# The due time of four early loads of w2 in a planned schedule: 240 becomes 300

## The chip, the core and the metric

One core of a Trainium2 chip runs the whole kernel; the metric is the device time of one execution in microseconds (us), lower is better. The time before is the median of 3 executions, 1378.37 us (1377.45 to 1378.69).

## What is computed

`x` is 2048 x 1024 in float32. Two sublayers follow each other, each behind an adaptive layer norm:

```python
h = _layernorm(x) * (1 + ca) + sa
x = x + ga * Real(DFT_seq(DFT_hidden(h)))          # first half
h = _layernorm(x) * (1 + cb) + sb
y = _layernorm(h)
x = x + gb * (gelu(y @ w1 + b1) @ w2 + b2)         # second half; w1: 1024 x 3584, w2: 3584 x 1024
```

The six rows sa ... gb are `silu(c) @ w_mod`.

## The kernel before

**The work.** The function `fast` does the first half with folded Fourier matrices and the second half as a Strassen-like scheme: w1 and w2 are cut into 14 pairs of columns or rows, and each product of a 2 x 2 block of such operands is made of 7 products, numbered m = 0 to 6 and taken in the order 0, 1, 2, 4, 3, 6, 5. Every operand is split into a high and a low float16 part, and one product is 12 matmuls of 128 x 512 (three passes by four). "gemm3 g" is the product with pair g of w1 (line 3628, 7 products, then a gelu), "gemm4 v" the one with pair v of w2 (line 3742, two blocks of 7 products, added up in SBUF). After the first gemm3 products the program is: gemm3 0, 1, 2, gemm4 0, gemm3 3, 4, gemm4 1 and so on up to gemm4 13.

**Preparing w1 and w2.** Before pair g of w1 or v of w2 can be used, its raw rows are loaded, four squares with a sum on ScalarE (line 3311), an all-reduce on GpSimd (L3323) and small VectorE instructions (L3319 to 3341) find its scale, and then 14 or so instructions split it: the high part on ScalarE (L2379), the low part (L2391) and combinations (L2405) on VectorE. The same lines split the gelu's output ("hid g"). Their third operand tells them apart: `s1c` is w1, `s2c` is w2, `shc` is hid. Operands for the first three pairs of w1 are made early, stored in HBM (`fw`), and loaded back ("reloads": L3480 for pairs 0 and 1, L3487 for pair 2) when their places come free. For pair 0 of w2 the rows are loaded twice: by `early2` (L3494, four loads of 512 KB) into a place that is free early, and only the squares read them; and by `raw2(0, q)` (L3497, four loads of 512 KB) into the place from which they are split. The raw rows of pairs 3 and 4 of w1 come by L3491 (four loads of 256 KB).

**What else runs there.** The end of the first half and the second half's layer norms overlap with this. A tile i of 128 rows is made by PE (L3046, L3058), assembled by VectorE (L3068, L3073), gets its residual (L3138 and L3139 for the last four tiles, whose x came by L3101), is stored to the output by SP (L3148, "x1 i"), goes through squares on ScalarE (L3120), small root steps (L2620, L2621, L2626 to 2629), two VectorE scalings (L3158, L3162) and a ScalarE scaling (L3171), is transposed on PE (L3181, "turn i"), copied (L3185) and split (L3211 high, L3220 low, L3233 combinations); GpSimd stores the splits of the second half of the tiles ("z", L3226, `fzc`). The pieces of the last eighth ("z7") pass through the place into which `raw2(1, q)` (L3296, rows of pair 1 of w2) is loaded next. L2894 and L2926 load w_mod's columns and b2 for the row gb, and L2900 multiplies it.

**How the order is set.** Nothing is ordered by hand: tasks with an engine, an assumed cost, dependences and a due time stand in streams, and a planner emits each engine's program in its own idea of time. Each engine then runs its program strictly in order, SP too, which issues all its loads and stores in the emitted order and waits at each for what it needs. Among a queue's tasks that are ready at once the planner takes the one with the earlier due time (`pick_first`). So a due time moves not only its own task, but all that is planned behind it, on all engines.

```python
for g, n in ((3, 2), (3, 3), (4, 0), (4, 1)):
    load(("raw1", g, n), f, [("P", 15), ("Q", 15)], 0.75, "rw2", 250.0)      # L3491
for q in range(4):
    load(("early2", q), f, [("P", 15), ("Q", 15)], 1.5, "rw3", 240.0)        # L3494
for q in range(4):
    load(("raw2", 0, q), f, [("turn", 13)], 1.5, "rw2", 240.0)               # L3497
```

P 15 and Q 15 are the products of the last tile of the first half.

Of the kernel before, what the change touches and what calls it, by code (L numbers as in the profile page):

```python
# [17 lines left out]
P = 128  # L18
# [1973 lines left out]
def fast(ctx, tc, x, cre, cim, dre, dim, w1, b1, w2, b2, c, wm, out):  # L1992
# [29 lines left out]
    def FA(off, *dims, p0=0, pn=P):  # L2022
        return view(arena32, off, dims, p0, pn)
# [104 lines left out]
    def raw1(g, n):  # L2128
        return at(raw1_at(g, n), 512)

    def raw2(v, q):
        return at(O_K + 4 * q, 1024).rearrange("p (s x) -> p s x", s=2)
# [314 lines left out]
    def add(stream, eng, cost, fn, deps=(), key=None, due=0.0, tag=None):  # L2447
        t = Task(eng, cost, fn, deps, key)
        push(stream, tag or stream, [t], due)
        return t.key  # L2450
# [38 lines left out]
    def load(name, f, deps=(), cost=1.4, stream="ld", due=0.0):  # L2489
        return add(stream, "dma", cost, f, deps, name, due)  # L2490
# [362 lines left out]
    for cls in range(2):  # L2853
        f = lambda cls=cls: gp.memset(FA(SPB[cls], (1, 1026), pn=64), 0.0)
# [228 lines left out]
    for n in range(2):  # L3083
        f = lambda n=n: gp.memset(FA(QS[n] + 256, (1, 1)), 0.0)
# [288 lines left out]
    def early2(q):  # L3373

        return at(144 + 4 * q, 1024).rearrange("p (s x) -> p s x", s=2)
# [114 lines left out]
    for g, n in ((3, 2), (3, 3), (4, 0), (4, 1)):  # L3490
        f = lambda g=g, n=n: sp.dma_start(raw1(g, n), w1[g, :, PLACE.index(n), :])  # L3491
        load(("raw1", g, n), f, [("P", 15), ("Q", 15)], 0.75, "rw2", 250.0)
    for q in range(4):
        f = lambda q=q: sp.dma_start(early2(q), w2[0:2, :, q, :].rearrange("j p x -> p j x"))  # L3494
        load(("early2", q), f, [("P", 15), ("Q", 15)], 1.5, "rw3", 240.0)
    for q in range(4):
        f = lambda q=q: sp.dma_start(raw2(0, q), w2[0:2, :, q, :].rearrange("j p x -> p j x"))  # L3497
        load(("raw2", 0, q), f, [("turn", 13)], 1.5, "rw2", 240.0)
# [523 lines left out]
def kernel(tc, *args):  # L4022
    odd = fast(tc, *args)
    with tc.If(odd > 0):
        general(tc, *args)
# [46 lines left out]
```

## Time and profile before

| what | value |
|---|---|
| median of 3 executions | 1378.37 us |
| profiled execution | 1377.23 us |
| its span, first to last instruction | 1375.4 us |
| TensorE matmul (PE) busy | 1291.3 us, 94% |
| VectorE (DVE) busy | 1088.4 us, 79% |
| ScalarE (ACT) busy | 746.6 us, 54% |
| moved to and from HBM | 306.22 MB, mean 223 GB/s |
| mean granted TensorE clock | 0.972 |

All times of the profile count from the first instruction. The execution lies 1.8 us outside the span (1377.23 - 1375.4). A row of a timeline gives start, length, engine, line, operation, and in brackets the idle time of the engine just before it and what ended that. PE is the matmul engine, SP's queue (SPq) issues loads and stores; a row of SPq is the issue, not the transfer. "x12" counts instructions merged in a row.

### The profile page before, as it was taken

The numbers are of one execution on the slowest core, as the hardware profiler recorded it, in microseconds if no ns is written. First come the engines' busy times: TensorE is split into PE (matmuls) and PEld (weight loads), VectorE is DVE, ScalarE is ACT, GpSimd is POOL, SyncE is SP. The second block draws the span as 40 slices with busy tenths as digits, with TensorE's granted clock in tenths as the row PEclk, the third lists the DMA queues.
The fourth block names the chain that finished last, engine by engine and source line by source line (L and its number), as shares of the span: only waits on it lengthen the run. The fifth ranks groups of instructions, "written<-read, shape, count | busy, mean of one in ns | idle before, by whom it ended". The sixth has DMA issues, their size and how long they took to land.

```text
span 1375.4 us, 17329 instructions
## 1 busy us (share of the span) xinstructions
PE 1291.3 (94%) x6081; PEld 622.9 (45%) x6081; DVE 1088.4 (79%) x1623; ACT 746.6 (54%) x1188; POOL 265.1 (19%) x426
## 2 busy tenths in 40 slices
PE   5888899777989999999999999999999999999997
PEld 1445466543434444444444444444444444444443
DVE  5888789998588999898989996566685858687695
ACT  4476557877667747474746433256545353636330
POOL 2000010102102000000000000254553433553201
PEclk9888899998999999999999999999999999999999
DMA  9777046569536957575453555999797878786524
GB/s 368 307 250 231 1 169 169 133 194 381 218 145 200 320 146 226 171 204 187 153 184 130 200 205 223 262 349 338 252 318 240 296 264 294 268 306 235 176 81 111
DMA packets 109754, 306.22 MB, mean 223 GB/s; under 512 B 14076, under 2 KB 14076, under 8 KB 107736
## 3 DMA queue, kind: packets, MB, share of 16 engines
q1 hardware_dynamic: 76776, 197.73, 40.5%
q0 software_dynamic: 32880, 107.29, 25.9%
q8 instruction: 49, 0.80, 0.2%
q14 instruction: 49, 0.40, 0.1%
HBM read 220.03 MB, written 84.93 MB: 222 GB/s over the span
## 4 chain that ended last, share of the span: by engine, by line
PE 67%; DVE 9%; ACT 4%; issue 2%; DMA 2%; SPq 0%; POOL 0%; DVEq 0%; ACTq 0%; POOLq 0%
PE ps L3742 34%; PE ps L3628 32%; ACT arena L2379 1%; DVE arena L2391 1%; DVE arena L3220 1%; DVE arena L2405 1%; DVE arena L3162 1%; PE ps L3046 1%; DVE arena L3233 1%; DMA arena<-fw 1%; DMA fzc<-arena 1%; ACT arena L3211 1%; DVE arena L3792 0%; DMA arena<-in_w_dram 0%; PE ps L3058 0%
## 5 line engine op out<-in xcount | busy, mean ns | idle before, releaser
L3628 PE MATMUL ps<-arena 128*128 128x512 f16 x2352 | 515.5, 381 | 9.4 <-DMA arena<-fw 4.8
L3742 PE MATMUL ps<-arena 128*128 128x512 f16 x2352 | 513.2, 380 | 8.0 <-ACT arena L3782 6.2
L3628 PEld LDWEIGHTS <-arena 128*128 128x128 f16 x2352 | 230.8, 98 | 289.9 <-issue 10.8
L3742 PEld LDWEIGHTS <-arena 128*128 128x128 f16 x2352 | 230.7, 98 | 288.3 <-issue 12.0
L3792 DVE SCALAR_TENSOR_TENSOR arena<-ps,i4c,arena 128x1024 f32<-128x1024 f32 x179 | 229.5, 1282 | 104.9 <-PE ps L3742 100.4
L2379 ACT ACTIVATE arena<-arena,shc 128x512 f16<-128x512 f32 (+1 forms) x115 | 115.8, 1017 | 137.2 <-DVE arena L2405 80.3
L2391 DVE SCALAR_TENSOR_TENSOR arena<-arena,shc 128x512 f16<-128x512 f32 (+1 forms) x115 | 129.0, 1121 | 29.6 <-ACT arena L2379 29.2
L2405 DVE TENSOR_TENSOR arena<-arena 128x512 f32<-128x512 f32 (+1 forms) x196 | 148.5, 764 | 3.7
L3533 ACT ACTIVATE arena<-arena 128x512 f32<-128x512 f32 (+5 forms) x148 | 91.2, 617 | 108.8 <-DVE arena L3542 84.8
L3647 ACT ACTIVATE arena<-arena,b1s,i1c 128x512 f32<-128x512 f32 x78 | 63.4, 813 | 90.0 <-DVE arena L3654 88.1
L2379 ACT ACTIVATE arena<-arena,s1c 128x512 f16<-128x512 f32 (+1 forms) x70 | 60.9, 886 | 66.5 <-DVE arena L2405 42.2
L3654 DVE TENSOR_TENSOR arena<-arena,ps 128x512 f32<-128x512 f32 x78 | 53.4, 685 | 52.4 <-PE ps L3628 51.7
L3542 DVE TENSOR_TENSOR arena<-arena 128x256 f32<-128x256 f32 x240 | 87.9, 421 | 1.7 <-DMA arena<-in_cre_dram 1.7
L3323 POOL PARTITION_ALL_REDUCE sums<-sums x21 | 10.4, 501 | 405.0 <-DVE sums L3319 405.0
L3559 POOL DMA_DIRECT2D arena<-in_cim_dram x99 | 54.5, 551 | 92.3 <-ACT arena L3533 86.1
L2391 DVE SCALAR_TENSOR_TENSOR arena<-arena,s1c 128x512 f16<-128x512 f32 (+1 forms) x70 | 65.8, 958 | 5.0 <-ACT arena L2379 4.9
L3559 POOL DMA_DIRECT2D arena<-in_cre_dram x99 | 54.6, 552 | 68.3 <-ACT arena L3533 50.9
L3650 ACT ACTIVATE arena<-ps 128x512 f32<-128x512 f32 x78 | 45.8, 588 | 35.8 <-PE ps L3628 35.6
L2391 DVE SCALAR_TENSOR_TENSOR arena<-arena,s2c 128x1024 f16<-128x1024 f32 x49 | 62.0, 1279 | 0.9 <-ACT arena L2379 0.9
L3046 PE MATMUL ps<-arena 128*128 128x256 f16 (+3 forms) x400 | 51.7, 290 | 10.1 <-DVE arena L3073 10.1
L2900 PE MATMUL ps<-arena,scol 128*128 128x512 f32 x128 | 58.3, 602 | 0.3 <-ACT arena L2915 0.3
L2379 ACT ACTIVATE arena<-arena,s2c 128x1024 f16<-128x1024 f32 x49 | 55.0, 1137 | 5.8 <-DVE arena L2405 5.8
(204 smaller groups left out, 1230.7 us busy)
## 6 DMA issues: line engine op xcount, KB each, us to landing
fw<-arena SPq DMA_DIRECT2D x71, 512.0 KB, 5.0
arena<-fw SPq DMA_DIRECT2D x119, 256.0 KB, 4.9
arena<-fw SPq DMA_DIRECT2D x49, 512.0 KB, 7.0
arena<-in_cre_dram POOLq DMA_DIRECT2D x96, 256.0 KB
arena<-in_cim_dram POOLq DMA_DIRECT2D x96, 256.0 KB
arena<-in_wm_dram SPq DMA_DIRECT2D x32, 512.0 KB, 7.5
arena<-in_w_dram SPq DMA_DIRECT2D x32, 512.0 KB, 6.4
arena<-in_w_dram SPq DMA_DIRECT2D x56, 256.0 KB, 4.5
```

The lines of the kernel that those rows point to most:

```text
L2379: act.activation(o[m][0], q(j), AF.Copy, **sc)
L2391: dve.scalar_tensor_tensor(o[m][1], q(j), scale, o[m][0], op0=ALU.mult, op1=ALU.subtract)
L2405: dve.tensor_tensor(q(d), q(a), q(b), op=op)
L2900: pe.matmul(bank((6 if n < 3 else 4) + h), scol[:, k : k + 1].to_broadcast([P, P]), FA(o + 512 * h, (1, 512)), start=k == 0, stop=k == 7,)
L3046: pe.matmul(PA(pb + o, (1, w)), l, r, start=n == 0, stop=n == len(mm_) - 1)
L3533: f = lambda: act.activation(sq(a), sq(a), AF.Square, accum_out=csum[0:pn, n : n + 1])
L3542: dve.tensor_tensor(a[:, o::2], a[:, o::2], b[:, o::2], op=op)
L3559: return lambda t: gp.dma_start(t[0:pn], v)
L3628: pe.matmul(ps.rearrange("p (k t) -> p k t", k=4), w1c[:, m, s, a, d * P : (d + 1) * P], zc(m)[:, b, :, d, :], start=(start and d == 0 and ...
L3647: act.activation(dst, src, AF.Gelu_apprx_tanh, scale=inv, bias=b1s[:, 2 * p + j : 2 * p + j + 1])
L3742: pe.matmul(t[:, j], hidc[:, c_, m, a, k * P : (k + 1) * P], w2c[:, m, c_, w], start=(start and c_ == 0 and n == 0), stop=(c_ == 1 and n = ...
L3792: lambda: dve.scalar_tensor_tensor(dst, ps[b], inv, dst, op0=ALU.mult, op1=ALU.add), kp[b],
```

## The change

One number: the due time of the four early loads of w2's rows goes from 240 to 300, behind that of the raw rows of w1 (250) and of all other loads that are planned there.

```diff
     for q in range(4):
         f = lambda q=q: sp.dma_start(early2(q), w2[0:2, :, q, :].rearrange("j p x -> p j x"))
-        load(("early2", q), f, [("P", 15), ("Q", 15)], 1.5, "rw3", 240.0)
+        load(("early2", q), f, [("P", 15), ("Q", 15)], 1.5, "rw3", 300.0)
```

No instruction is added to or taken from PE; the planner's orders change on all engines from P 15 on. Three places matter.

**SP's queue around the reloads.** These are SP's rows from the load of the last x tiles (L3101) on: first before, then of the change. L3491 are w1's raw rows, L3494 the early rows of w2, L3148 the stores of x1 13 and then x1 14 and 15, L3487 and L3480 the reloads, L2894 and L2926 the loads for gb.

```order
L3494 DMA arena_65<-in_w_dram 128x2x512
L3101 DMA arena_65<-in_x_dram 128x2x1024
L3494 DMA arena_65<-in_w_dram 128x2x512 x3
L3491 DMA arena_65<-in_w_dram 128x512 x2
L3148 DMA out_dram<-arena_65 128x1024
L3491 DMA arena_65<-in_w_dram 128x512 x2
L3487 DMA arena_65<-fw_2_78 128x1024
L3480 DMA arena_65<-fw_0_76 128x1024
L2894 DMA arena_65<-in_wm_dram 128x1024 x5
L3480 DMA arena_65<-fw_1_77 128x1024
L3148 DMA out_dram<-arena_65 128x1024
L2926 DMA arena_65<-in_b_dram 128x1024
```

```order
L3491 DMA arena_65<-in_w_dram 128x512 x2
L3494 DMA arena_65<-in_w_dram 128x2x512 x3
L3148 DMA out_dram<-arena_65 128x1024
L3494 DMA arena_65<-in_w_dram 128x2x512
L3487 DMA arena_65<-fw_2_78 128x1024
L3148 DMA out_dram<-arena_65 128x1024
L3480 DMA arena_65<-fw_0_76 128x1024
L2894 DMA arena_65<-in_wm_dram 128x1024 x5
L3480 DMA arena_65<-fw_1_77 128x1024
L3480 DMA arena_65<-fw_0_76 128x1024
L3480 DMA arena_65<-fw_1_77 128x1024
L2926 DMA arena_65<-in_b_dram 128x1024
```

The second piece begins one load after the first: ahead of it stand two L3491 and the same L3101. The early rows of w2 now follow w1's raw rows, and, which the due time does not say, the store of x1 14 has moved ahead of the reload for product 2 of gemm3 0 (the first L3480 here), and two more reloads (product 3) ahead of b2. Behind these rows the store of x1 15 stands ahead of the next reloads, L3487 x2 and L3480 x6, where before it stood behind the first four L3480 of them.

**ScalarE around the four squares of w2 pair 0.** These are ACT's rows from L3171 of tiles 10 and 11 on, before and then of the change. L3311 are the squares, L3928 the copies of gemm3 0's products, L3120 the squares of tiles 12 and 13.

```order
L3311 ACTIVATE arena_65,sums_2197<-arena_65 128x1024
L3211 ACTIVATE arena_65<-arena_65 128x2x512
L3211 ACTIVATE arena_65<-arena_65 128x512
L3120 ACTIVATE arena_65,lns_21_141<-arena_65,lns_21_141 128x1024 x2
L3185 ACTIVATE arena_65<-ps 128x1024
L3928 ACTIVATE arena_65<-ps 128x512
L3211 ACTIVATE arena_65<-arena_65 128x2x512
L3185 ACTIVATE arena_65<-ps 128x1024
L2620 ACTIVATE lns_21_141<-lns_21_141,eps_13_114 128x2
L2621 ACTIVATE lns_21_141<-lns_21_141,eps_13_114 128x2
L3311 ACTIVATE arena_65,sums_2197<-arena_65 128x1024 x3
L3120 ACTIVATE arena_65,lns_21_141<-arena_65,lns_21_141 128x1024 x2
```

```order
L3120 ACTIVATE arena_65,lns_21_141<-arena_65,lns_21_141 128x1024
L3185 ACTIVATE arena_65<-ps 128x1024
L3928 ACTIVATE arena_65<-ps 128x512
L2620 ACTIVATE lns_21_141<-lns_21_141,eps_13_114 128x2
L2621 ACTIVATE lns_21_141<-lns_21_141,eps_13_114 128x2
L3211 ACTIVATE arena_65<-arena_65 128x2x512
L3311 ACTIVATE arena_65,sums_2282<-arena_65 128x1024
L3928 ACTIVATE arena_65<-ps 128x512
L3120 ACTIVATE arena_65,lns_21_141<-arena_65,lns_21_141 128x1024 x2
L2620 ACTIVATE lns_21_141<-lns_21_141,epsz_115 128x2
L2621 ACTIVATE lns_21_141<-lns_21_141,epsz_115 128x2
L3311 ACTIVATE arena_65,sums_2282<-arena_65 128x1024
```

One square and not four stands ahead of the second L3120 x2, and the copy of product 2 (the second L3928), which waits for PE, has moved ahead of them; before it stood behind them.

**VectorE ahead of gemm4 0.** These are the DVE rows that end with the first L3792, which adds up gemm4 0's second product, before and then of the change.

```order
L2391 SCALAR_TENSOR_TENSOR arena_65<-arena_65,s1c_147 128x512
L3654 TENSOR_TENSOR arena_65<-arena_65,ps 128x512
L2391 SCALAR_TENSOR_TENSOR arena_65<-arena_65,shc_149 128x2x512
L2391 SCALAR_TENSOR_TENSOR arena_65<-arena_65,s1c_147 128x512
L2405 TENSOR_TENSOR arena_65<-arena_65 128x1024
L2405 TENSOR_TENSOR arena_65<-arena_65 128x512
L2391 SCALAR_TENSOR_TENSOR arena_65<-arena_65,s2c_151 128x2x512 x2
L2405 TENSOR_TENSOR arena_65<-arena_65 128x1024 x2
L2391 SCALAR_TENSOR_TENSOR arena_65<-arena_65,s2c_151 128x2x512 x3
L3792 SCALAR_TENSOR_TENSOR arena_65<-ps,i4c_152,arena_65 128x2x512
```

```order
L2391 SCALAR_TENSOR_TENSOR arena_65<-arena_65,s2c_151 128x2x512
L3654 TENSOR_TENSOR arena_65<-arena_65,ps 128x512
L2405 TENSOR_TENSOR arena_65<-arena_65 128x1024 x2
L3319 TENSOR_REDUCE sums_2710<-sums_2710 128x1
L3327 TENSOR_SCALAR sums_2710<-sums_2710 128x1
L3349 COPY f2c_146<-sums_2710 128x1
...
L2391 SCALAR_TENSOR_TENSOR arena_65<-arena_65,s2c_151 128x2x512 x3
L3792 SCALAR_TENSOR_TENSOR arena_65<-ps,i4c_152,arena_65 128x2x512
L2391 SCALAR_TENSOR_TENSOR arena_65<-arena_65,s1c_147 128x512 x2
L2405 TENSOR_TENSOR arena_65<-arena_65 128x512
```

Three instructions for pair 3 of w1 (two `s1c` and the last L2405 of 512) no longer stand between or ahead of the last parts of w2 pair 0; they come behind L3792. On ACT the two `s1c` go behind the first L3782 (which takes gemm4 0's first product out of PSUM) in the same way, and only three instead of five `s2c` stand together right ahead of L3782. On PE, product 4 of gemm3 0 goes ahead of turn 13, products 0 and 1 of gemm3 1 go behind turn 14, and product 3 of gemm3 1 goes behind turn 15.

## Prediction

> **What bounds the kernel now.** I began with the busy shares by stretch (start:end, length, then PE, PEld, DVE, ACT and POOL busy with instruction counts, granted clock, DMA share, GB/s).
>
> ```profile
> span 1375.4 us, 17329 instructions
> ...
> 300.00:320.00 20.00, 15.56 (x59) 7.94 (x58) 16.84 (x25) 15.62 (x24) 4.84 (x7) 0.82 1.00 349
> 320.00:340.00 20.00, 14.51 (x53) 6.74 (x51) 19.35 (x39) 16.78 (x26) 5.92 (x9) 0.95 1.02 365
> 340.00:360.00 20.00, 18.25 (x82) 8.53 (x83) 8.69 (x19) 8.53 (x16) 2.61 (x4) 0.88 0.89 348
> 400.00:500.00 100.00, 94.18 (x423) 41.93 (x423) 85.62 (x133) 67.02 (x88) 14.28 (x20) 0.97 0.78 239
> 500.00:700.00 200.00, 200.00 (x928) 90.68 (x927) 180.64 (x245) 117.38 (x154) 9.84 (x15) 1.00 0.60 187
> ```
>
> From 500 us on PE has no idle time, so what the change saves or loses before that passes to the end one to one. From 300 to 340 the DMA engines are full (1.00, 1.02) while PE is not. Then I read PE's timeline and its waits.
>
> ```profile
> 312.04 5.28 PE L3628 MATMUL ps<-arena 128*128 128x512 f16 x12 [3.29 <-DVE arena L3073]
> ...
> 322.07 2.76 PE L3628 MATMUL ps<-arena 128*128 128x512 f16 x12 [1.09 <-DMA arena<-fw]
> 324.67 3.60 PE L2900 MATMUL ps<-arena,scol 128*128 128x512 f32 x8
> ...
> 329.58 5.32 PE L2900 MATMUL ps<-arena,scol 128*128 128x512 f32 x12
> 336.93 1.09 PE L3181 MATMUL ps<-ident,arena 128*128 128x128 f32 x8 [2.03 <-ACT arena L3185]
> 341.75 17.25 PE L3628 MATMUL ps<-arena 128*128 128x512 f16 x72 [3.73 <-DMA arena<-fw]
> ...
> 404.50 20.87 PE L3742 MATMUL ps<-arena 128*128 128x512 f16 x84 [6.21 <-ACT arena L3782]
> ```
> ```profile
> 444.19 26.22 PE L3628 MATMUL ps<-arena 128*128 128x512 f16 x120 [0.70 <-ACT arena L3650]
> 471.04 5.34 PE L3628 MATMUL ps<-arena 128*128 128x512 f16 x24 [0.62 <-ACT arena L3650]
> 476.21 24.12 PE L3742 MATMUL ps<-arena 128*128 128x512 f16 x111
> ```
>
> The last big stop is 6.21 us ahead of 404.50 (product 2 of gemm4 0); the one ahead of 341.75 is the wait for the reload of product 4 of gemm3 0. A full-speed matmul is 24.12/111 = 0.217 us, a product 2.61. The 72 at 341.75 should take 15.6 and take 17.25 (1.6 lost), the 84 at 404.50 18.25 and take 20.87 (2.6 lost), and the 12 at 312.04 take twice their time: a stop of 3.3 us or more costs 1.6 to 2.6 on top.
>
> Why the 6.21? The queue that PE waited for:
>
> ```profile
> 398.97 2.48 DVE L2405 TENSOR_TENSOR arena<-arena 128x1024 f32<-128x1024 f32 x2
> 401.41 3.68 DVE L2391 SCALAR_TENSOR_TENSOR arena<-arena,s2c 128x1024 f16<-128x1024 f32 x3
> ```
> ```profile
> 400.23 3.23 ACT L2379 ACTIVATE arena<-arena,s2c 128x1024 f16<-128x1024 f32 x3 [3.10 <-DVE arena L2405]
> 403.36 1.09 ACT L3782 ACTIVATE arena<-ps,i4c 128x1024 f32<-128x1024 f32 x1
> ```
>
> L3782 frees gemm4 0's first bank. It stands on ACT behind the last splits of w2 pair 0, these wait for combinations on DVE, and DVE is late because it prepared hid 0, hid 1, w2 pair 0 and part of pair 3 of w1 in one run.
>
> **Term A: PE's entry into gemm4 0.** No PE instruction is added, so I count PE's work from T, the start of product 4 of gemm3 0 (341.75 before). In the changed order 11 products (28.7), three transpositions of 8 (turn 13 now lies behind T; 1.0 each by the row at 336.93, 3.0) and the slow start (1.6), then 7 products of gemm3 2 (18.3) and 2 of gemm4 0 (5.2) follow: product 2 of gemm4 0 at T + 56.8. This holds if DVE and ACT keep up, which I take them to do: L3782 has three splits, not five, right ahead, and three pair-3 instructions on DVE go behind, two narrow L2391 and one narrow L2405 (next starts follow some 0.1 us inside the lengths of these rows, so 0.66 + 0.66 + 0.6, about 1.9 us):
>
> ```profile
> 391.17 0.75 DVE L2391 SCALAR_TENSOR_TENSOR arena<-arena,s1c 128x512 f16<-128x512 f32 x1
> ...
> 437.29 0.68 DVE L2405 TENSOR_TENSOR arena<-arena 128x512 f32<-128x512 f32 x1
> ```
>
> Before, the same place was reached at 404.50 + 2.6 = 407.1 in full-speed terms. With T unchanged A is 407.1 - 398.55 = 8.5.
>
> **T itself.** These rows of SP's queue, with the landing that the chain of waits gives, and one of ACT and DVE:
>
> ```profile
> 317.78 0.38 SPq L3480 DMA_DIRECT2D arena<-fw  x1
> ...
> 328.49 0.34 SPq L3148 DMA_DIRECT2D out_dram<-arena  x1
> ...
> 332.44 4.29 SPq L3480 DMA_DIRECT2D arena<-fw  x4
> 337.59 0.34 SPq L3148 DMA_DIRECT2D out_dram<-arena  x1
> ```
> ```profile
> 332.44 9.26 DMA arena<-fw
> ```
> ```profile
> 317.36 0.60 ACT L3928 ACTIVATE arena<-ps 128x512 f32<-128x512 f32 x1 [2.52 <-PE ps L3628]
> ...
> 323.48 1.13 ACT L3120 ACTIVATE arena<-arena,lns 128x1024 f32<-128x1024 f32 x1
> ...
> 325.87 0.29 ACT L2620 ACTIVATE lns<-lns,epsz 128x2 f32<-128x2 f32 x1
> ```
> ```profile
> 326.30 0.16 DVE L2626 RECIPROCAL lns<-lns 128x2 f32<-128x2 f32 x1
> ...
> 328.98 0.68 DVE L3073 TENSOR_TENSOR arena<-ps,arena 128x512 f32<-128x512 f32 x1
> ...
> 331.50 1.22 DVE L3138 TENSOR_TENSOR arena<-arena 128x1024 f32<-128x1024 f32 x1
> ...
> 335.74 1.22 DVE L3139 SCALAR_TENSOR_TENSOR arena<-arena 128x1024 f32<-128x1024 f32 x1
> ```
>
> The four early loads and the four L3491 change places, which by bytes is nothing (both sets still stand ahead of all reloads). But the store of x1 14 (issued 328.49) now precedes the reload of product 2 (317.78), and the store of x1 15 (337.59) that of product 4 (332.44). A store is 512 KB, 1.5 us at the 349 GB/s of its stretch. So product 2, which waits for its reload alone, comes about 1.8 us later (one issue, one store): 323.9 to 326.5. Its copy now stands ahead of the squares L3120 that began at 323.48, so tiles 12 to 15 shift by about 3 us: copy 0.5, two squares 2.3, roots 0.4, the small DVE steps 1.0, L3073 0.6, L3138 1.1, L3139 1.2 end the tile 15 that x1 15 waits for, 7.1 us behind product 2, and with the issues ahead the reload of product 4 goes out 8.4 behind it: 334.9 instead of 332.44. It needs no more waiting than before, and two reloads (product 3) have left its front. Lower bound for T: turn 12 waits for the same chain (5.5 us behind product 2), then 1.1 and the 5.32 of L2900: 326.5 + 11.9 = 338.4. Upper bound: product 2 starts after a stop of 2.9 us; if that costs what the 3.29 at 312.04 did, it ends at 329.2, the reload goes out at 337.6 and with the 9.26 lands at 346.9. Since the DMA engines are full either way I take the old T plus one store, T = 343.25, and keep 338.4 and 346.9. **A is 407.1 - 400.05 = 7.0.**
>
> The page "TensorE: Matmul & The Clock Gate" of the Trainium skill (Part 1) says that the clock falls to half after an idle window of about 3.4 us; by that the 2.9 us cost nothing more and the upper end of T is 344.3. The trace has halving at 3.29 and none at 2.03 (336.93), so no row here decides it.
>
> **Term B: DVE up to gemm4 1.** Rows of the next piece, and SP's wait:
>
> ```profile
> 422.32 1.83 DVE L3220 TENSOR_TENSOR arena<-arena 128x1024 f16<-128x1024 f32 x2
> ...
> 441.04 0.16 DVE L3319 TENSOR_REDUCE sums<-sums 128x1 f32<-128x4 f32 x1 [3.08 <-ACT ps L3311]
> ...
> 474.62 1.28 DVE L2391 SCALAR_TENSOR_TENSOR arena<-arena,s2c 128x1024 f16<-128x1024 f32 x1
> ...
> 479.00 1.28 DVE L3792 SCALAR_TENSOR_TENSOR arena<-ps,i4c,arena 128x1024 f32<-128x1024 f32 x1 [1.11 <-PE ps L3742]
> ```
> ```profile
> 439.86 1.03 ACT L3311 ACTIVATE ps<-arena 128x1024 f32<-128x1024 f32 x1 [1.05 <-DMA arena<-in_w_dram]
> ```
> ```profile
> SPq L3296 <- DMA fzc<-arena: 8.3, 2, 7.8
> ```
>
> The rows of w2 pair 1 can be loaded only when z7's stores have left the same place; z7 ends on DVE at 424.1, the last square waits for its load until 439.86, and DVE stops until 441.04. From there to the end of w2 pair 1's last part (475.82) DVE works almost without a gap, 34.8 us. z7's last pieces stand behind the fourth L3782 in both orders, so they move with PE, by A: DVE resumes at 441.04 - 7.0 = 434.0. But in the changed order more stands between: counted in the two orders, one wide and one narrow L2391, two narrow L2405 and one norm's five small steps of some 0.15 (1.2 + 0.66 + 1.2 + 0.75 = 3.8). So the last part ends at 434.0 + 34.8 + 3.8 = 472.6, and the first evacuation of gemm4 1, which stands behind it on DVE (L3792, 1.2), at 473.8. PE wants that bank for product 2 of gemm4 1 at 400.05 + 26 products (67.8) + 5.2 = 473.05. It waits 0.75, and a stop so short shows no slow clock. Before, there were 0.70 and 0.62 of such stops in this piece; I leave them in. B is -0.5 to -0.75; bounds: 0, and -7.7, if z7's stores land no earlier than before (441.04 + 38.6 + 1.2 = 480.8 against 473.05). I take -0.5, nearer the first, as the chain to z7 goes through PE.
>
> **Sum:** 7.0 - 0.5 = 6.5 us. The profiled execution of 1377.23 (span 1375.4 + 1.8) would become 1370.7; it lies 1.1 below the median, so the median of 1378.37 becomes 1371.9.
>
> **Rivals.** *The gain is given back at gemm4 1.* DVE, 86% busy from 400 to 500, prepares w2 pair 1 later than before, and w1 pair 4 and hid 2 ahead of it. For it: the waits through z7's stores have 7.8 us in one piece. Against it: DVE still idles 3.08 there. With B at 5 to 7.7 the time is 1376.5 to 1379, no change.
> *Slower: the reload of product 2.* Each us that it lands late is passed on, through the copy, the squares, tile 15, x1 15 and SP, to the reload of product 4. It landed 4.3 us after its issue (317.78 to 322.07). If it takes the 9.26 that the other took, product 2 starts at 327.4, ends slow at 332.7, the next reload goes out at 341.1 and lands at 350.4; with the last x tiles' load another 1 to 2 us late, T is 352 and A is -1.7. From T = 352.5 on (6.5 + 2.75 later than my T) it is a loss that counts: 1381 to 1382. For it: DMA share 1.00. Against it: only 512 KB more stand ahead.
> The page "DMA: Bandwidth & Descriptors" (Queues, rings and completion order) of the Trainium skill says that each engine consumes a queue's descriptors in ring order and takes turns between queues; it speaks for this rival. By it the store ahead costs at least its bytes; the 9.26 at 332.44 agrees with a queue, 4.3 at 317.78 with a short one.
> *The loads go earlier than T needs.* If two reloads fewer in front and the idle SP let product 4's land at once, T is 338.4 and A 11.9; B stays, since z7 and DVE move with PE: 1367.
>
> **How the numbers follow.** Forecast and its surroundings (T 340 to 346) 0.60, early T 0.10, gain given back 0.16, slower 0.14. A measurement tells about 0.2% (2.75 us) from no change. Faster 0.70, the same 0.16, slower 0.14. The range takes T from 338.4 to 346.9 with B from 0 to -5: 1366.5 to 1379.5.
>
> **What would show it.** Right: no stop of 6 us ahead of product 2 of gemm4 0, PE there at about 400; the wait for the reload of product 4 ends at 340 to 346; product 2 of gemm3 0 starts 1 to 3 us later; the last square of w2 pair 1 starts about 433; PE stops under 1.5 us at product 2 of gemm4 1. Wrong: a PE stop over 3 us between 405 and 480, or after 500; T beyond 350; a stop at gemm4 0 as before, which would mean that DVE's work and not its order made it.

## The result, and the profile after

The change makes the kernel faster: a median of 1369.96 us (1367.97 to 1370.92, 4 executions) against 1377.91 of the kernel before (1377.30 to 1378.69, 4 executions), ratio 0.9949 with a 95% interval of 0.9931 to 0.9967. The forecast was 1371.9. The profiled execution took 1370.08 us. On a second chip, with more executions, the kernel before spread from 1370.1 to 1379.2 (31, median 1375.0), the change from 1368.5 to 1373.0 (10, median 1370.4): ratio 0.9957, 0.9941 to 0.9973. The gain is real, and it is nearer to 5 us than to the 8 of the first medians.

The profile of the change, busy shares by stretch (columns as in the prediction):

```profile
span 1368.1 us, 17330 instructions
...
300.00:320.00 20.00, 12.11 (x47) 5.87 (x45) 19.41 (x33) 13.89 (x21) 4.84 (x7) 0.81 1.03 375
320.00:340.00 20.00, 16.66 (x40) 6.96 (x40) 11.98 (x20) 13.66 (x23) 2.76 (x4) 0.76 0.84 295
340.00:360.00 20.00, 17.68 (x88) 8.77 (x89) 13.54 (x29) 15.83 (x22) 6.21 (x10) 1.00 1.02 371
400.00:500.00 100.00, 97.24 (x452) 43.86 (x451) 86.97 (x134) 63.91 (x84) 15.09 (x21) 1.00 0.79 229
500.00:700.00 200.00, 200.00 (x928) 90.62 (x927) 182.65 (x249) 122.65 (x161) 9.34 (x15) 1.00 0.62 195
```

From 400 to 500 PE is busy 97.24 instead of 94.18 and the clock is whole. PE's timeline at the places of the prediction (the first row is the last product of tile 15):

```profile
292.59 4.13 PE L3046 MATMUL ps<-arena 128*128 128x257 f16 x24 [3.15 <-DVE arena L3073]
...
320.93 5.29 PE L3628 MATMUL ps<-arena 128*128 128x512 f16 x12 [3.87 <-DMA arena<-fw]
...
341.29 2.76 PE L3628 MATMUL ps<-arena 128*128 128x512 f16 x12 [1.50 <-DMA arena<-fw]
...
361.04 5.34 PE L3628 MATMUL ps<-arena 128*128 128x512 f16 x24 [1.84 <-ACT arena L3928]
...
398.62 31.24 PE L3742 MATMUL ps<-arena 128*128 128x512 f16 x144 [0.29 <-ACT arena L3782]
429.70 36.42 PE L3628 MATMUL ps<-arena 128*128 128x512 f16 x168
...
474.06 6.22 PE L3742 MATMUL ps<-arena 128*128 128x512 f16 x28 [2.76 <-DVE arena L3792]
```

The 6.21 ahead of product 2 of gemm4 0 is 0.29, and the 144 matmuls behind it run at full speed. The two small stops of the kernel before (0.70 in gemm3 3, 0.62 in gemm3 4) are gone too. Two new stops stand at 361.04 and at 474.06 (product 2 of gemm4 1).

**A trap in this comparison.** Up to the products of tile 15 both programs are the same, yet this profile is 2.45 us early there. Here is the same row of the kernel before, and then of a repetition of the change (the second view ended at 300 and holds 21 of the 24 matmuls):

```profile
295.04 5.30 PE L3046 MATMUL ps<-arena 128*128 128x257 f16 x24 [3.15 <-DVE arena L3073]
```
```profile
295.64 4.66 PE L3046 MATMUL ps<-arena 128*128 128x257 f16 x21 [3.15 <-DVE arena L3073]
```

Over the 14 profiles of this study that row starts anywhere from 290.17 to 295.64, whichever kernel runs. So I count each profile from there: "the stretch" is the span less the start of that row, and a place "at +46.7" lies 46.7 us behind it. Before, the stretch is 1375.4 - 295.04 = 1080.36 (repeated: 1080.31); of the change 1368.1 - 292.59 = 1075.51 (repeated: 1371.1 - 295.64 = 1075.46). **By these profiles, two of each kernel, the change is worth 4.85 us**; the other 2.45 of the 7.3 between the two spans belong to the execution. One thing stays open: the fastest execution of the kernel before on the second chip has a span of 1368.3, and with a stretch of 1080.3 the shared row would lie at 288.0 there, earlier than in any profile. So some executions of the kernel before probably have a shorter stretch than its two profiles.

### The profile page after: what moved, and what is told of

Its sections match the earlier page's. It is cut to its first block, busy times and chain, and to the rows that moved or that the text cites. A ratio compares the mean times of both kernels' runs of the same rounds, so it can differ in the third digit from the quotient of the medians.

```text
span 1368.1 us, 17330 instructions
## 1 busy us (share of the span) xinstructions
PE 1285.2 (94%) x6081; PEld 620.1 (45%) x6081; DVE 1089.1 (80%) x1623; ACT 748.2 (55%) x1188; POOL 263.8 (19%) x426
## 4 chain that ended last, share of the span: by engine, by line
PE 67%; DVE 10%; DMA 3%; ACT 2%; issue 2%; SPq 1%; POOL 0%; DVEq 0%; POOLq 0%; ACTq 0%
PE ps L3742 34%; PE ps L3628 31%; DVE arena L2391 2%; DVE arena L3220 1%; DVE arena L3162 1%; DVE arena L2405 1%; ACT arena L2379 1%; DMA arena<-in_w_dram 1%; PE ps L3046 1%; DVE arena L3233 1%; DMA arena<-in_wm_dram 1%; PE ps L3058 1%; DMA frow_gbb<-arena 0%; DVE arena L3654 0%; PE ps L3181 0%
## 5 line engine op out<-in xcount | busy, mean ns | idle before, releaser
L3792 DVE SCALAR_TENSOR_TENSOR arena<-ps,i4c,arena 128x1024 f32<-128x1024 f32 x179 | 229.4, 1282 | 103.0 <-PE ps L3742 101.0
L2405 DVE TENSOR_TENSOR arena<-arena 128x512 f32<-128x512 f32 (+1 forms) x196 | 148.9, 764 | 3.7
L3654 DVE TENSOR_TENSOR arena<-arena,ps 128x512 f32<-128x512 f32 x78 | 53.4, 685 | 51.6 <-PE ps L3628 50.9
L2900 PE MATMUL ps<-arena,scol 128*128 128x512 f32 x128 | 61.5, 630 | 2.7 <-DMA arena<-in_wm_dram 2.4
L3311 ACT ACTIVATE ps<-arena 128x1024 f32<-128x1024 f32 x46 | 46.7, 1016 | 19.0 <-DMA arena<-in_w_dram 9.6
```

Of the source, the lines that this page charges most:

```text
L2405: dve.tensor_tensor(q(d), q(a), q(b), op=op)
L2900: pe.matmul(bank((6 if n < 3 else 4) + h), scol[:, k : k + 1].to_broadcast([P, P]), FA(o + 512 * h, (1, 512)), start=k == 0, stop=k == 7,)
L3792: lambda: dve.scalar_tensor_tensor(dst, ps[b], inv, dst, op0=ALU.mult, op1=ALU.add), kp[b],
```

## The experiments

My theory after the result: DVE's order ahead of the first evacuation of gemm4 0 made the stop of 6.21, the pieces of pair 3 above all, and part of the gain is given back at gemm4 1, where DVE has too much to do. The rivals: the loads alone make the gain through T; or the difference is in the execution.

In the table, T is the start of product 4 of gemm3 0; "entry" is the start of product 2 of gemm4 0; the stops are those at product 2 of gemm4 0 and of gemm4 1, with a star where PE ran at half clock for some us behind it. Ratios are to the kernel before on the same chip, whose medians beside e1 to e4, e5 to e8 and e9 to e12 were 1375.0, 1374.7 and 1375.1. Where no entry is given, no stop marks the place in PE's merged rows.

| run | median us (executions) | ratio, 95% | T | entry | stops | stretch |
|---|---|---|---|---|---|---|
| before | 1377.91 (4) | | +46.71 | +109.46 | 6.21*, none | 1080.36 |
| change | 1369.96 (4) | 0.9949, 0.9931 to 0.9967 | +48.70 | +106.03 | 0.29, 2.76 | 1075.51 |
| e1 | 1370.41 (10) | 0.9957, 0.9941 to 0.9973 | +47.80 | +105.98 | 0.28, 2.75 | 1075.46 |
| e2 | 1373.46 (10) | 0.9989, 0.9969 to 1.001 | +45.75 | +105.46 | 3.87*, 2.75* | 1078.26 |
| e3 | 1376.46 (10) | 1.001, 0.9992 to 1.0029 | +48.43 | +110.80 | 5.18*, none | 1080.17 |
| e4 | 1372.29 (10) | 0.9974, 0.9956 to 0.9992 | +47.50 | | none, 3.23* | 1075.50 |
| e5 | 1365.89 (4) | 0.9929, 0.9909 to 0.995 | +46.51 | +104.23 | 0.29, none | 1071.03 |
| e6 | 1366.89 (4) | 0.9929, 0.9904 to 0.9954 | +48.96 | | none, none | 1073.57 |
| e7 | 1377.30 (1) | | +47.06 | +109.65 | 6.21*, none | 1080.31 |
| e8 | 1370.64 (9) | 0.9964, 0.9948 to 0.9981 | +47.55 | +104.85 | 0.28, 2.75* | 1075.90 |
| e9 | 1372.39 (10) | 0.9967, 0.9951 to 0.9984 | +47.10 | +105.31 | 0.29, 2.75* | 1076.33 |
| e10 | 1368.81 (5) | 0.9947, 0.9924 to 0.997 | +48.72 | +106.28 | 0.29, none | 1073.19 |
| e11 | 1366.43 (5) | 0.9942, 0.9919 to 0.9965 | +45.71 | | none, none | 1071.80 |
| e12 | 1366.90 (6) | 0.9947, 0.9928 to 0.9965 | +45.17 | | none, none | 1070.56 |

**e1, the change again** (no edit).

> The changed kernel once more, to see how much of its 7.3 us between the two profiles is the change. Up to the products of tile 15 both programs are the same, yet the profile of the change stood 2.45 us earlier there (SP's load at the same place of the queue 297.06 against 299.51, PE L3046 292.59 against 295.04). Theory: that part is a difference of one execution and not of the change, so the same place comes between 292.5 and 295.1 in this profile, and behind it the rows are the same to 0.5 us: the stop ahead of product 2 of gemm4 0 under 0.5, the one at product 2 of gemm4 1 2.5 to 3.0, the median 1369.5 to 1372. Rival: the place is early in all profiles of the change, so that the change itself makes those 2.45 us.

The early place is at 295.64, late as in the kernel before, while the stops at gemm4 0 and gemm4 1 and the stretch repeat to 0.05 us. So the 2.45 us are the execution's (the row came 0.54 later than I had allowed; its spread is wider than I thought).

**e2, the kernel before with pair 3 of w1 late.**

```diff
-    push_w1(3)
...
-            push_w1(g + 2)
+            if g != 2:
+                push_w1(g + 2)
         else:
             v = k
+            if v == 0:
+                push_w1(3)
+                push_w1(4)
```

> The kernel before (due 240), with one thing alone from the changed order: the splits of pair 3 of w1 are planned only when gemm4 0 starts, so that DVE's three narrow pieces of it (0.66 + 0.66 + 0.6, 1.9 us) and ACT's two lie behind the splits of w2 pair 0. Nothing ahead of gemm3 2 moves. Theory (DVE's work ahead of the first evacuation sets the stop, and these pieces are 1.9 of it): the stop of 6.21 ahead of product 2 of gemm4 0 becomes 4.2 to 4.6, the slow start behind it stays (20.9 for 84), and the time is 1375.5 to 1376.5. Rival 1 (it was the order of these pieces alone): the stop is under 1 us and the time 1369 to 1371. Rival 2 (pair 3 has no part in it, the gain came from the loads): stop over 5.5, time 1377.5 to 1379.

PE's timeline of e2:

```profile
338.39 15.70 PE L3628 MATMUL ps<-arena 128*128 128x512 f16 x72
...
398.10 32.75 PE L3742 MATMUL ps<-arena 128*128 128x512 f16 x144 [3.87 <-ACT arena L3782]
...
475.04 15.24 PE L3742 MATMUL ps<-arena 128*128 128x512 f16 x62 [2.75 <-ACT ps L3311]
```

The stop falls by 2.34 to 3.87, a little more than the 1.9 of the three pieces, and the slow start stays in part (32.75 for 144, where full speed takes 31.24). So pair 3 is one part of it, neither all (rival 1) nor nothing (rival 2). The entry is 4.0 earlier, more than the stop, because this execution did not wait for the reload of product 4 at all (first row, no bracket): on DVE 1.7 of the 4.0 is there ahead of the place of the pieces already (the L3654 there starts at 385.00, or +92.36; in the kernel before at 389.08, or +94.04), and 2.3 is gained from there to L3792. Half of the 4.0 does not reach the end: at gemm4 1 a stop of 2.75 with half clock stands where before there was none. The stretch gains 2.1; by its median e2 cannot be told from the kernel before (0.9969 to 1.001).

**e3, the change with pair 3 early.**

```diff
-    push("w1", "n1_3", w1_norm(3), due[3, 3] - 20.0)
-    push_w1(3)
+    for k_, d_ in (("n1", w1_norm(3)), ("w1", w1_tasks(3))):
+        push("w1", k_ + "_3", d_, 260.0)
+    push("w1", "n1_4", w1_norm(4), due[3, 4] - 20.0)
```

> The changed kernel, with the splits of pair 3 of w1 ahead of w2 pair 0's again (by their due time, 260): five narrow pieces and a norm of five small steps are then on DVE ahead of the last splits of w2 pair 0. Everything up to gemm3 2 is as in the change. Theory (DVE reaches the first evacuation of gemm4 0 just when PE wants it, 0.29 us late): each of these pieces is passed on, 3 to 3.5 us; the stop at product 2 of gemm4 0 is 3 to 4 and is followed by a slow start, 1.6 to 2.6 more, and the time 1373.5 to 1376. Rival (DVE has idle time there, since the change gives it more of it): stop under 1, time 1369.5 to 1371.

DVE, and then PE, of e3:

```profile
383.01 0.15 DVE L3319 TENSOR_REDUCE sums<-sums 128x1 f32<-128x2 f32 x1 [1.05 <-ACT ps L3311]
383.76 0.15 DVE L3327 TENSOR_SCALAR sums<-sums 128x1 f32<-128x1 f32 x1 [0.59 <-POOL sums L3323]
...
388.62 0.75 DVE L2391 SCALAR_TENSOR_TENSOR arena<-arena,s1c 128x512 f16<-128x512 f32 x1 [0.30 <-ACT arena L2379]
...
389.89 0.75 DVE L2391 SCALAR_TENSOR_TENSOR arena<-arena,s1c 128x512 f16<-128x512 f32 x1
390.55 2.01 DVE L2405 TENSOR_TENSOR arena<-arena 128x512 f32<-128x512 f32 x3
...
398.74 3.68 DVE L2391 SCALAR_TENSOR_TENSOR arena<-arena,s2c 128x1024 f16<-128x1024 f32 x3
402.33 1.28 DVE L3792 SCALAR_TENSOR_TENSOR arena<-ps,i4c,arena 128x1024 f32<-128x1024 f32 x1
```
```profile
401.83 20.18 PE L3742 MATMUL ps<-arena 128*128 128x512 f16 x84 [5.18 <-ACT arena L3782]
```

The theory holds, and the price is higher than I said: 5.18 and not 3 to 4, since DVE also waits at the new places (1.05 and 0.59 for pair 3's norm, 0.30 ahead of its first piece). With all loads as in the change, its whole gain is gone: the stretch is 1080.17, and by the median e3 is level with the kernel before (0.9992 to 1.0029) and clear of the change (0.9941 to 0.9973). **So the loads alone do not make the gain; without the order of pair 3's work behind w2 pair 0's there is none.** That the stretch is just that of the kernel before is chance: e3 has five pieces ahead, with waits, where the kernel before had three, and its entry is 1.3 later, but it loses less afterwards (20.18 for 84 instead of 20.87, and one stop of 0.67 instead of the 0.70 and 0.62).

**e4, gbb's product early.** In the change ACT's copy L3928 waits for the store of gbb. The chain of waits of the change has this store, issued by GpSimd, under way (first row), and then what follows it:

```profile
353.64 6.67 DMA frow_gbb<-arena
...
360.39 0.61 ACT arena L3928
...
361.04 4.04 PE ps L3628 x18
```

```diff
-            k = add("rowd", "dve", 1.25, lambda: dve.tensor_tensor(w, w, g, op=ALU.mult), [l, ("rowe", 3)], None, 246.0)
+            k = add("rowd", "dve", 1.25, lambda: dve.tensor_tensor(w, w, g, op=ALU.mult), [l, ("rowe", 3)], None, 200.0)
```

> The changed kernel, with the row gbb's product (L2928 on DVE, 1.2 us) planned as soon as its operands are there (its due time 246 becomes 200), as it stood in the order before; its store then goes out some 10 us earlier. In the changed kernel the second product of gemm3 1 waits 1.84 us (361.04) for a copy on ACT that waits for this store to land, and DVE stops 4.49 there. Theory: both go; PE gains 1.5 to 1.8 there, and since DVE's stop goes too, DVE does not hold gemm4 0 (stop under 0.5) and the time is 1368 to 1368.7. Rival: DVE has 1.2 us more to do ahead of turn 13 and gemm4 0, so the 1.84 comes back as a stop at gemm4 0 or gemm4 1: time 1369.5 to 1371.

PE of e4, from gemm4 0 on:

```profile
393.31 36.66 PE L3742 MATMUL ps<-arena 128*128 128x512 f16 x168
...
474.64 25.60 PE L3742 MATMUL ps<-arena 128*128 128x512 f16 x110 [3.23 <-DVE arena L3792]
```

The theory fails, the rival wins. The 1.84 is gone and gemm4 0 has no stop (168 in one row); product 2 of gemm4 1 starts 1.83 earlier (+179.64 against +181.47). But the stop there grew to 3.23 and the clock halved behind it (25.60 for 110, full speed 23.9): 1.7 us lost, and the stretch is the same, 1075.50. The median, 1372.29, lies above the rival's range too.

**e5, the first evacuation of gemm4 1 ahead of the last splits.** In the change the planner places all splits of w2 pair 1 ahead of gemm4 1's first evacuation on DVE:

```profile
430.80 0.16 DVE L3319 TENSOR_REDUCE sums<-sums 128x1 f32<-128x4 f32 x1 [1.02 <-ACT ps L3311]
...
469.13 3.68 DVE L2391 SCALAR_TENSOR_TENSOR arena<-arena,s2c 128x1024 f16<-128x1024 f32 x3
472.72 2.67 DVE L3792 SCALAR_TENSOR_TENSOR arena<-ps,i4c,arena 128x1024 f32<-128x1024 f32 x2
```

```diff
-            need(f"w2_{v}", f"hid{2 * v}", f"hid{2 * v + 1}")
+            need(*([f"w2_{v}"] if v != 1 else []), f"hid{2 * v}", f"hid{2 * v + 1}")
...
+                if v == 1 and blk == 0:
+                    emitted(*(("w2", v, n) for n in ORDER[: slot + 2]))
+                    for _ in range(6 if slot == 0 else 0):
+                        force(streams["w2"], streams["w2"][0])
...
+                if (v, blk, slot) == (1, 0, 3):
+                    push_w1(5)
+                    push_w1(6)
...
-            push_w1(g + 2)
+            if g not in (3, 4):
+                push_w1(g + 2)
```

> The changed kernel, with DVE's order at gemm4 1 alone altered: the first evacuation (L3792 of product 0) is planned ahead of the last three splits of w2 pair 1, not behind them, each later split just ahead of the product that reads it, and the splits of pair 5 of w1 start after product 4 of gemm4 1. Nothing is added or left out. The measure is the stretch from the last product of tile 15 (PE L3046, 292.59 in the profile of the change) to the end: 1375.51 of the change, 1375.46 - 300 in the same terms of its repetition, that is 1075.5 in both. Theory (the 2.76 stop at product 2 of gemm4 1 is made by the three splits, 3.68, ahead of that evacuation): the stop becomes 0.2 to 1.2, the stretch 1073.0 to 1074.0, the median about 1368.5. Rival (DVE has too much work altogether before the end of gemm4 1, in whatever order): a stop of 1.5 or more comes back at a later product of gemm4 1 and the stretch stays at 1075 to 1075.6.

(In this text 1375.51 and "1375.46 - 300" should read 1075.51 and 1075.46.) DVE and PE of e5 at gemm4 1; the edit moves L3792 to line 3799:

```profile
462.46 2.48 DVE L2405 TENSOR_TENSOR arena<-arena 128x1024 f32<-128x1024 f32 x2
464.86 1.28 DVE L3799 SCALAR_TENSOR_TENSOR arena<-ps,i4c,arena 128x1024 f32<-128x1024 f32 x1
466.06 1.27 DVE L2391 SCALAR_TENSOR_TENSOR arena<-arena,s2c 128x1024 f16<-128x1024 f32 x1
467.25 1.28 DVE L3799 SCALAR_TENSOR_TENSOR arena<-ps,i4c,arena 128x1024 f32<-128x1024 f32 x1
```
```profile
461.74 36.67 PE L3742 MATMUL ps<-arena 128*128 128x512 f16 x168
```

The stop is gone altogether and nothing comes back later: 168 matmuls in one row. Against the 2.76 that this can give, the stretch is 4.5 shorter; the rest comes from an earlier entry (+104.23 for +106.03), with T at +46.51. e10 shows whether that belongs to the kernel.

**e6, both edits of e4 and e5.**

> The two edits together: gbb's product early (as in the run before, where PE gained 1.8 by the second product of gemm3 1, then stood 3.23 at product 2 of gemm4 1 and ran slow behind it, 25.60 for 110 matmuls, so that the stretch behind tile 15 was 1075.5 as in the change) and the first evacuation of gemm4 1 ahead of the last splits. Theory (the 1.8 was lost only at gemm4 1): the stop falls to 0.5 to 1.6, without a slow start, and the stretch is 1071.0 to 1072.5; the median about 1367. Rival (w2 pair 1 itself is late, not the evacuation, since its rows come through z7): the stop is 2.5 or more again and the stretch 1074.5 to 1075.6.

The theory holds at gemm4 1, which has no stop and begins 423.2 behind T (in e5 425.1, in e10 424.9). Yet the stretch is 1073.57, since PE stops 1.61 us much later, ahead of the third product of another gemm4:

```profile
909.32 31.24 PE L3742 MATMUL ps<-arena 128*128 128x512 f16 x144 [1.61 <-ACT arena L3789]
```

Just ahead of it DVE waited four times, up to 1.37 us, for loads of one input (`in_cre_dram` in the views). Without this stop the stretch would be 1071.96, inside the theory's range. No other profile has it, e12 with the same two edits included, so it belongs to this execution as far as the record shows.

**e7, the kernel before again** (no edit).

> The kernel before once more, since its runs on this chip lie between 1370 and 1379, and since another kernel with its order up to gemm4 0 did not wait for the reload of product 4 of gemm3 0 at all (in the first profile of before it waited 3.73). Theory (the landing of that reload varies from one execution to the next by some us while the DMA engines are full, and DVE's run ahead of gemm4 0 does not follow it): the wait at product 4 is anything from 0 to 4, product 2 of gemm4 0 comes 109 to 110 behind the last product of tile 15 (109.46 in the first profile) with a stop of 5.5 to 10, and the stretch from there to the end is 1079.9 to 1080.9. Rival (DVE follows the reload): with no wait at product 4 the place is 105 to 106 and the stretch 1076 to 1077.

The profile repeats the first one (wait at product 4 of 4.09, entry +109.65, stretch 1080.31). A case without the wait did not come, so the question is not answered here; e2, which has it in another order of DVE, says that DVE follows (1.7 us earlier there).

**e8, the store of x1 14 behind the reload of product 2.**

```diff
-            store("x1", i, lambda n=n, i=i: sp.dma_start(o_s[i // 8, i % 8], y[:, n]), k)
+            push("x1", "st_x1", [Task("st", 0.0, lambda n=n, i=i: sp.dma_start(o_s[i // 8, i % 8], y[:, n]), [k, ("w1", 0, 2)] if i == 14 else [k], ("st", "x1", i))])
```

> The changed kernel, with the store of x1 14 put back behind the reload of product 2 of gemm3 0 in SP's queue (it also moves behind two of the five loads of w_mod's columns). This takes away the one thing that my estimate of T had as delayed. Theory (the store costs its bytes): product 2 of gemm3 0 comes 1 to 2 us earlier against the last product of tile 15 (28.3 in the profile of the change, 29.1 in its repetition), and product 4 with it (48.7, 47.8); but DVE and not T sets the start of gemm4 0 (between the two profiles T differs by 0.9, and product 2 of gemm4 0 lies at 106.0 in both), so the stretch behind tile 15 stays at 1075.2 to 1075.7. Rival (what T gains is passed on to gemm4 0): stretch 1073.5 to 1074.5.

PE of e8:

```profile
321.75 4.45 PE L3628 MATMUL ps<-arena 128*128 128x512 f16 x12 [2.02 <-DMA arena<-fw]
...
342.85 4.19 PE L3628 MATMUL ps<-arena 128*128 128x512 f16 x12 [3.09 <-DMA arena<-fw]
...
475.58 32.87 PE L3742 MATMUL ps<-arena 128*128 128x512 f16 x144 [2.75 <-DVE arena L3792]
```

Product 2 comes at +26.45 (change +28.34, e1 +29.10), 1.9 to 2.7 earlier, where the bytes of the store are some 1.5 us by the prediction's estimate. This place varies by itself: in the other eight profiles with the store ahead of the reload it lies at +27.48 to +29.60, in the three with the order of before at +27.03 to +27.79. So the direction is shown, the size only roughly. By the page "DMA: Bandwidth & Descriptors" (Queues, rings and completion order) of the Trainium skill each DMA engine consumes a queue's descriptors in ring order, and this agrees. T gains only 0.25 to 1.15 of it, as product 4 now waits 3.09 for its own reload. The stretch stays near (1075.90), but not for my reason: the entry did come 1.2 earlier (+104.85), and was lost to half clock behind an equal stop at gemm4 1 (32.87 for 144, 1.6 too long). Without that loss the stretch would be 1074.3, inside the rival's range: what was gained ahead did reach gemm4 0.

**e9, e5's control: pair 5 held back alone** (the last two parts of e5's diff).

> The control of the first kernel with an early evacuation at gemm4 1: the changed kernel, where only the splits of pair 5 of w1 start after product 4 of gemm4 1; the first evacuation stays behind all splits of w2 pair 1. Theory (that order is the cause of the stop of 2.75 at product 2 of gemm4 1): the stop stays, 2.6 to 2.9, and the stretch from the last product of tile 15 to the end is 1075.4 to 1077.3 (the upper end if PE's clock halves behind the stop, which it did behind equal stops of two other kernels at 1.7 us). Rival (the early kernel gained by holding pair 5 back): stop under 1.

The stop is 2.75: the order of the evacuation made e5's gain at gemm4 1, not the holding back.

**e10, e5's kernel again.**

> The changed kernel with the first evacuation of gemm4 1 ahead of the last splits, once more and timed together with the next. Its first profile had no stop over 1 us behind 337, product 4 of gemm3 0 at 46.5 behind the last product of tile 15, and 1071.03 in all behind that place; the kernel with gbb's product early as well had product 4 at 48.96 and 1073.57. Theory (with both stops gone, what is left of the stretch is fixed by the landing of product 4's reload, T, and is T + 1024.5): the stretch is T + 1024.3 to T + 1025.0 here too, whatever T is. Rival (the two differ by gbb's product): 1070.8 to 1071.3 at any T.

As the theory has it: T at +48.72, stretch 1073.19, T + 1024.47 (e5: T + 1024.52). That e6 has T + 1024.61 is chance, by its late stop. So e5's edit is worth 2.3, and its further 2.2 went with an earlier T; the last section says why T need not be the cause. The 9 executions of this kernel on two chips lie between 1363.0 and 1370.0.

**e11 and e12, column 5 of w_mod ahead of turn 12**, in e5's kernel and in e6's. The edit:

```diff
-            add("rowp", "pe", 2 * FP, f, deps, ("wru", m), (39.0, 39.0, 39.5, 245.0)[n])
+            add("rowp", "pe", 2 * FP, f, deps, ("wru", m), 230.0 if m == 29 else (39.0, 39.0, 39.5, 245.0)[n])
...
-            load(("w1", g, m), f, ([("turn", 5)] if m < 2 else [("turn", 11)] if m < 4 else [*hidend, ("wru", 31)]) + [("w1s", g, q) for q in range(7)], cost=0.7, stream="wl" if m < 2 else "wl2" if m < 4 else "wl4", due=200.0)
+            load(("w1", g, m), f, ([("turn", 5)] if m < 2 else [("turn", 11)] if m < 4 else [*hidend, ("wru", 29 if m == 4 else 31)]) + [("w1s", g, q) for q in range(7)], cost=0.7, stream="wl" if m < 2 else "wl2" if m < 4 else "wl4", due=200.0)
```

> The same, with one more edit: on PE the product with w_mod's column 5 (L2900, two of its matmul pairs) is planned ahead of turn 12, where PE waits 2.2 us for ScalarE, because the reload of product 4 of gemm3 0 needs the place of that column; and in SP's queue the reloads for pair 2 (L3487) go behind. Theory: the reload is issued as soon as the store of x1 15 has gone out, 1 to 2 us earlier, T comes at 44 to 46.5 instead of 46.5 to 49, and the stretch with it: 1069 to 1071. Rival (the store of x1 15, which waits for tile 15 on DVE, holds the reload anyway, and the landing takes what it takes): T and the stretch as before, 1071 to 1073.6; with more of DVE's work ahead of gemm4 0 in the new order a stop there instead.

> All three edits: gbb's product early, the first evacuation of gemm4 1 ahead of the last splits, and column 5 ahead of turn 12. Theory: as the kernel without gbb's edit, less what is left of the stop at the second product of gemm3 1 (0.96 in its profile): stretch 1068.5 to 1070.5, the median 1363 to 1366. Rival: DVE becomes the bound at gemm4 0 (stop of 1 to 3 there) and the stretch is 1071 to 1073.

SP's queue, and then PE, of e11:

```profile
333.62 0.34 SPq L3148 DMA_DIRECT2D out_dram<-arena  x1
334.06 3.70 SPq L3480 DMA_DIRECT2D arena<-fw  x6
```
```profile
338.51 4.45 PE L3628 MATMUL ps<-arena 128*128 128x512 f16 x12 [2.17 <-DMA arena<-fw]
```

T moves as expected, to +45.71 and +45.17. The stretches, 1071.80 and 1070.56, miss my ranges by 0.8 and 0.06: in e11 product 4 starts at half clock behind its 2.17 (4.45 for 12) and 1.39 are left at the second product of gemm3 1; in e12 a stop of 1.39 stands in gemm3 3. By the stretch both beat the change by 3.7 to 5.0 us; by ratio (0.9942 and 0.9947 to the kernel before) they beat the kernel before surely, the change (0.9949, 0.9957) only within overlapping intervals, and against e5, e6 and e10 (0.9929, 0.9929 and 0.9947) their ratios show no gain. e12's median, 1366.90, misses its range of 1363 to 1366 too.

## Why the prediction was right, step by step

**What bounds it, and the place of the loss: right.** The stop of 6.21 was DVE's order, with L3782 behind the splits. e3 shows it from one side (pair 3 early in the changed kernel gives all back), e2 from the other (pair 3 late in the kernel before takes 2.3 off the stop).

**Term A, 7.0: measured 6.0.** Before, the entry was reached at +109.46 + 2.6 = +112.06 in full-speed terms; now at +106.03. Of the 6.0, I put 2.3 down to pair 3's pieces (by e2's stop) and 2.6 to the half clock that no longer follows; the 1.1 that is left may be the rest of DVE's new order, which no run took apart. In the change the pieces of pair 3 stand just behind the evacuation, as the orders had it:

```profile
395.72 3.67 DVE L2391 SCALAR_TENSOR_TENSOR arena<-arena,s2c 128x1024 f16<-128x1024 f32 x3
399.31 1.27 DVE L3792 SCALAR_TENSOR_TENSOR arena<-ps,i4c,arena 128x1024 f32<-128x1024 f32 x1
400.50 1.40 DVE L2391 SCALAR_TENSOR_TENSOR arena<-arena,s1c 128x512 f16<-128x512 f32 x2
```

I had the entry at T + 56.8, it came at T + 57.3, by two errors of opposite sign: no slow start at T (2.76 for 12, I counted 1.6), but the 1.84 at the second product of gemm3 1, which I did not foresee. gbb's store moved behind in the order, and its landing of 6.67 stands ahead of a copy on ACT.

**T: right, by a path that varies.** Predicted 343.25, measured 341.29 + 2.45 = 343.74 in the clock of the profile of before. SP's rows and the landing, from the chain of waits:

```profile
314.06 0.38 SPq L3148 DMA_DIRECT2D out_dram<-arena  x1
314.53 0.40 SPq L3480 DMA_DIRECT2D arena<-fw  x1
...
333.64 0.34 SPq L3148 DMA_DIRECT2D out_dram<-arena  x1
...
335.40 5.69 SPq L3480 DMA_DIRECT2D arena<-fw  x6
```
```profile
335.40 5.84 DMA arena<-fw
```

Product 2 started at 320.93 + 2.45 = 323.4 (predicted 323.9) and ran at half clock behind its 3.87, so the reload of product 4 went out 14.5 behind its start, where I had 11 to 13.7; it then landed in 5.84 and not 9.26. The two offset each other: that T came out within 0.5 us is luck. The rule that I had weighed, of the page "TensorE: Matmul & The Clock Gate" (Part 1) of the Trainium skill, has the clock fall behind some 3.4 us without work. The 3.87 here agrees with it, the shorter stops of the last section do not.

**Term B, -0.5: measured -1.1, and the mis-sized step.** Product 2 of gemm4 1 starts at +181.47; before it was 24 matmuls behind 476.21, so at 481.4 or +186.4: 4.9 earlier, of A's 6.0. DVE resumed where I said (430.80 + 2.45 = 433.25, predicted 434.0). The step that failed is "DVE's 34.8 us plus 3.8": it took 42.0. The stretch of DVE from there to the last part, first before, then of the change (DVE is the number behind PE's and PEld's):

```profile
441.04:475.82 34.78, 33.46 (x155) 14.93 (x154) 33.50 (x50) 28.32 (x37) 6.42 (x8) 1.00 0.97 270
```
```profile
430.80:472.80 42.00, 40.50 (x188) 18.17 (x186) 38.17 (x61) 32.29 (x42) 6.75 (x9) 1.00 0.87 228
```

The work grew by 4.7 (38.17 - 33.50; I had 3.8), and the gaps by 2.5 (3.8 for 1.3), which I had left as they were: in the new order DVE waits for ScalarE's high parts (0.79 us at most) and for two of GpSimd's reductions (0.59 and 0.51). So PE stood 2.76 and not 0.75. Against that the 0.70 and 0.62 in gemm3 3 and 4, which I had left in, went.

**The sum.** 6.0 - 1.1 = 4.9 against my 6.5; the stretch says 4.85. The first two medians differ by 7.95, some 3 us more than that; from the median of 1378.37 that the forecast starts from, 4.85 would have given 1373.5, inside the range and 1.6 above the forecast. So the measured median lies 1.9 below the forecast by luck of the executions, and not because A or B was larger than I said. Two small errors of the working change nothing: T at 346.9 with B at -5 gives an upper end of 1380.0, not 1379.5; and PE does stop behind 500 us, for 0.43, 0.15 and 1.25 us near the end, in both kernels alike.

**The rivals.** The gain given back at gemm4 1 happened in part (2.76 of stop there, and all that e4 gained). The slower case did not: product 2's reload took 6.4 from its issue to the start of its product (314.53 to 320.93), not 9.26. T as early as 338.4 did not come in the change (+48.70 and +47.80, 342.8 to 343.7 in the clock of before).

## What to carry to other kernels

A due time in a planned schedule moves the order of engines far away; look there for what the engine that gates the next stage (here DVE ahead of an evacuation) has to do before it, and count its waits for other engines in the new order too, not only its instructions. An evacuation that is planned behind all operands of a stage holds the stage's third product; place it ahead of the operands that come later. And where executions differ ahead of the change, measure from the last instruction that both programs share.

## What the runs showed of the hardware

**Half clock behind short stops.** Behind a stop of 2.75 to 2.76 us after a long busy run PE kept full speed in two profiles (the change, e1) and fell to half in three (e2, e8, e9). The granted clock (third column from the right) behind the stop at 474.06 of the change, and behind the equal one at 475.58 of e8:

```profile
474.00:476.00 2.00, 1.94 (x9) 0.89 (x10) 1.90 (x4) 0.18 (x2) 0.00 (x0) 1.00 1.01 264
476.00:478.00 2.00, 2.00 (x11) 0.92 (x10) 2.00 (x4) 1.15 (x2) 0.00 (x0) 1.00 0.91 315
```
```profile
475.00:477.00 2.00, 1.42 (x4) 0.58 (x5) 1.90 (x3) 0.70 (x2) 0.00 (x0) 0.62 0.97 303
477.00:479.00 2.00, 2.00 (x7) 0.67 (x5) 1.83 (x3) 1.15 (x2) 0.00 (x0) 0.53 0.94 295
```

From product 2 of gemm4 1 to the end it is 894.0 us in the first case (1075.51 - 181.47; e1 the same) and 895.6 in e8 (1075.90 - 180.28) and e9 (1076.33 - 180.74): 1.6 us more. In pieces with several stops 2.02 (e8, the first of its rows above) and 2.17 (e11) were enough, each 4.45 for 12, while behind 2.23 in e12 PE ran at full speed (2.76 for 12). What decides between the like cases stays open.

**Landing of one reload.** That of product 4 made PE wait 0.47 to 4.09 us in 13 of the 14 profiles, which are of 11 kernels, and not at all in e2; in two profiles of one kernel it was 3.73 and 4.09 (before), 1.50 and 0.69 (the change), 2.59 and 1.39 (e5's). It does not fix the end alone. The stretch is T + 1024.5 in e5 and e10, but the change and e1 have the same stretch with T 0.9 apart. In the five profiles where the second product of gemm3 1 waits for gbb's store and the entry has no large stop (the change, e1, e5, e9, e10) the entry lies 37.6 behind that product, and the product starts 34.6 to 34.9 behind the end of product 2 of gemm3 0, against 19.8 to 20.6 behind T. In e8, where product 2 came earliest, ScalarE's copy there did not wait for the store. So T and the entry seem both to follow product 2, and with it its reload and its clock; no run tests this. Of the 6.9 between the two spans of e5's kernel (1361.2 and 1368.1), 2.2 lie in the stretch and 4.7 in the time up to tile 15 (290.17 and 294.91).
